# Edge rows of P by V stacked into shared groups, bounds moved between engines, first loads halved

## The chip, the cores and the metric

The kernel runs on one core of one Trainium2 chip. The time is that of one execution on the device, in microseconds (us), median of three runs. Engines are named as in the profile: PE (TensorE, matrix products, with PEld for its weight loads), DVE (VectorE), ACT (ScalarE), POOL (GpSimd) and SP (SyncE, which here only issues DMA transfers).

## The reference

Windowed attention with a few global tokens, then a two-layer network on its output. Batch 8, 8 heads, 512 local and 32 global tokens per batch, head width 64, model width 512, inner width 2048.

```
s_l = scale * concat(q_l k_g^T, where(|i-j| <= 32, q_l k_l^T, -1e9))
out_l = softmax(s_l) @ concat(v_g, v_l)
out_g = softmax(scale * q_g concat(k_g, k_l)^T) @ concat(v_g, v_l)
x = concat(out_g, out_l), heads side by side        # 8*544 tokens x 512
h = x @ w_in ;  g = h * tanh(softplus(h)) ;  out = g @ w_out
```

## The kernel before, in words

All large products are done in 16-bit pieces with float32 accumulation. An operand is scaled by a power of two, its high part is rounded to float16 and its low part (what is left) is a second float16; a product is then three 16-bit matmuls (high-high, high-low, low-high). The scale needs a bound on the operand, and each operand has its own way to get one: for W1 and W2 (`w_in`, `w_out`) PE sums squares by small products of a piece with itself into `w_s` (`w_stat`, L568); for V of batch 0, DVE takes the largest magnitude (`b_max`, L667 and L670); for V of later batches ACT sums magnitudes (L663). `w_bits` (L546 to L549) first rebuilds float32 words from the 64-bit words in which the weights come.

Attention goes by batch `b`, head pair `hp` and tile `t` of 128 query rows (four tiles for 512 rows). A tile needs keys of its own 128 rows, 32 rows on either side, and the 32 global rows. `scores` (L837) gives the products, `row_max` (L852, DVE) adds the mask and takes the row's largest, `expo` (ACT, L862 in batch 0, L865 with a row sum elsewhere) gives P. In batches from 1 on `p_hi` and `p_lo` split P into `ph`, a DMA transpose (`p_turn`, L637) writes `pt`, and `pv` (L954) multiplies `pt` by V: `vf` holds the tile's own V rows, `vb` the edge and global rows, which four small DMAs per head pair copy next to each other (`v_move`). Twelve matmuls serve a tile: two heads, two groups of rows, three products. In batch 0 PE itself transposes P (`p_pe`, L889, L897) and sums its rows by products with a column of ones (L960).

The network goes in 17 blocks of 256 tokens (two per batch, one for the global tokens) and 8 slices of the inner width: `h` (L1132 in block 0, L1142 after it), the function of h on ACT and DVE (`mish`, L1283 to L1293), its split into `GG` (L456, L1302), and the product with W2 into `o` (L1314, from block 4 on L1410). PSUM has two buffers for `h`: the third slice can start only when ACT has read the first. `w_split` (L456, L604) splits W1 and W2.

Nothing is scheduled on the chip: `Plan` lists all tasks, and a table `STEPS` gives the order in which they are written out, so each engine has one fixed order. `SECOND` lists the tasks that go to the second of two possible engines (mostly DVE in place of ACT). `FILL` says where unused products of a constant (`w_s<-consts`, L1721) are put ahead of a task; 73 stand in the program. All large DMAs, small moves and DMA transposes are issued by SP, in one order, from two helper lines (L445, L637). A tile is taken from a ring of buffers, in the order of the rings.

The lines that follow are those which the steps of the prediction touch.

Of the kernel before, what the change touches and what calls it, by code (L numbers as in the profile page):

```python
# [1800 lines left out]
```

## Time and profile before

| | us |
|---|---|
| median of three runs | 862.61 (862.17 to 863.95) |
| the profiled execution | 863.22 |
| its span in the trace | 861.4 |
| PE busy | 848.1 (98%) |
| DVE busy | 771.5 (90%) |
| ACT busy | 674.9 (78%) |
| POOL busy | 14.8 (2%) |

The span is what the trace covers; 1.8 us of the execution lie around it. A busy share is an average: an engine that is busy 78% of the span can be full in one stretch. The granted TensorE clock is 1.00 of full speed in all stretches read below. L numbers are lines of the kernel before.

### The profile page before, as it was taken

The numbers are of one execution on the slowest core, as the hardware profiler recorded it, in microseconds if no ns is written. First come the engines' busy times: TensorE is split into PE (matmuls) and PEld (weight loads), VectorE is DVE, ScalarE is ACT, GpSimd is POOL, SyncE is SP. The second block draws the span as 40 slices with busy tenths as digits, with TensorE's granted clock in tenths as the row PEclk, the third lists the DMA queues.
The fourth block names the chain that finished last, engine by engine and source line by source line (L and its number), as shares of the span: only waits on it lengthen the run. The fifth ranks groups of instructions, "written<-read, shape, count | busy, mean of one in ns | idle before, by whom it ended". The sixth has DMA issues, their size and how long they took to land.

```text
span 861.4 us, 23843 instructions
## 1 busy us (share of the span) xinstructions
PE 848.1 (98%) x9341; PEld 711.0 (83%) x9341; DVE 771.5 (90%) x2191; ACT 674.9 (78%) x1416; POOL 14.8 (2%) x29
## 2 busy tenths in 40 slices
PE   7999999999999999999999999999999999999998
PEld 5888866577777788888888888888888889888987
DVE  7999999998999999998999988899989998899771
ACT  5999998799998999987898888887687783444450
POOL 1010000000000000000000000000000000000000
PEclk9999999999999999999999999999999999999999
DMA  8889487878878586786766676677655454000001
GB/s 280 305 294 264 136 154 180 177 167 169 205 159 189 115 182 136 154 191 148 155 138 161 139 162 137 153 164 164 132 119 110 94 90 75 1 26 2 26 4 48
DMA packets 213841, 122.85 MB, mean 143 GB/s; under 512 B 172384, under 2 KB 181472, under 8 KB 213728
## 3 DMA queue, kind: packets, MB, share of 16 engines
q1 hardware_dynamic: 213728, 121.33, 60.6%
q8 instruction: 73, 1.20, 0.6%
q14 instruction: 40, 0.33, 0.1%
HBM read 65.84 MB, written 8.91 MB: 87 GB/s over the span
## 4 chain that ended last, share of the span: by engine, by line
PE 91%; DVE 4%; ACT 2%; DMA 2%; issue 1%; SPq 1%; DVEq 0%; ACTq 0%
PE h L1142 35%; PE o L1410 27%; PE o L1314 10%; PE U L954 5%; PE s L837 4%; PE h L1132 3%; PE h L1216 2%; PE g L1029 2%; PE gu L1090 1%; PE w_s L568 1%; DMA vl<-in_vm 1%; DMA wraw<-in_w 1%; DVE W L549 1%; DVE P L852 0%; SPq L445 0%
## 5 line engine op out<-in xcount | busy, mean ns | idle before, releaser
L1142 PE MATMUL h<-xx,W 128*128 128x256 f16 x2880 | 334.1, 273 | 0.8 <-ACT e L1283 0.8
L1142 PEld LDWEIGHTS <-W 128*128 128x128 f16 x2880 | 276.1, 98 | 37.6 <-issue 4.3
L1410 PEld LDWEIGHTS <-GG 128*128 128x128 f16 x2037 | 196.9, 98 | 23.1 <-issue 0.7
L1410 PE MATMUL o<-W,GG 128*128 128x256 f16 x1455 | 167.9, 273 | 0.0
L1302 DVE SCALAR_TENSOR_TENSOR GG<-e,c,GG 128x896 f16<-128x896 f32 (+1 forms) x129 | 134.5, 1047 | 6.3 <-ACT GG L456 5.0
L456 ACT ACTIVATE GG<-e,c 128x896 f16<-128x896 f32 (+1 forms) x103 | 98.9, 967 | 38.4 <-DVE e L1293 34.5
L1283 ACT ACTIVATE e<-h,c 128x512 f32<-128x512 f32 x128 | 85.8, 684 | 36.9 <-PE h L1142 23.7
L865 ACT ACTIVATE P<-P,nm 128x192 f32<-128x192 f32 (+1 forms) x224 | 102.4, 458 | 10.9 <-DVE nm L852 10.1
L852 DVE CUSTOM_DVE_ANT_0 P<-s,masks 128x192 f32<-128x192 f32 (+1 forms) x256 | 89.1, 366 | 6.9 <-PE s L837 6.3
L1314 PE MATMUL o<-W,GG 128*128 128x512 f16 x384 | 90.2, 379 | 0.0
L934 DVE SCALAR_TENSOR_TENSOR ph<-P,ph 128x384 f16<-128x384 f32 x168 | 69.2, 440 | 3.2 <-ACT ph L456 2.8
L954 PEld LDWEIGHTS <-pt 128*128 128x128 f16 (+1 forms) x1536 | 60.4, 98 | 10.0 <-issue 3.5
L1410 PE MATMUL o<-t,GG 128*128 128x256 f16 x582 | 67.8, 273 | 0.0
L1283 ACT ACT_TABLE_LOAD x49 | 62.9, 1283 | 5.6 <-DVE GG L1302 4.7
L1314 PEld LDWEIGHTS <-GG 128*128 128x128 f16 x384 | 35.3, 98 | 37.0 <-issue 1.6
L954 PE MATMUL U<-vf,pt 128*128 128x64 f16 x768 | 56.1, 193 | 0.0
L954 PE MATMUL U<-vb,pt 128*128 128x64 f16 (+1 forms) x768 | 55.9, 192 | 0.0
L1291 DVE TENSOR_TENSOR e<-e 128x256 f32<-128x256 f32 x104 | 43.5, 421 | 1.6
L865 ACT ACT_TABLE_LOAD x33 | 42.3, 1283 | 0.5
L865 ACT ACTIVATION_READ_ACCUMULATOR P<-P,nm 128x1 f32 x224 | 42.1, 188 | 0.0
L456 ACT ACTIVATE ph<-P 128x384 f16<-128x384 f32 (+1 forms) x101 | 38.9, 421 | 0.9 <-DMA pt<-ph 0.5
L696 ACT ACTIVATE mx<-mx 128x544 f32<-128x544 f32 x48 | 31.1, 648 | 9.3 <-DMA mx<-in_mxs 9.1
(231 smaller groups left out, 1242.3 us busy)
## 6 DMA issues: line engine op xcount, KB each, us to landing
mx<-in_mxs SPq DMA_DIRECT2D x48, 272.0 KB, 3.1
vl<-in_vm SPq DMA_DIRECT2D x32, 256.0 KB, 3.8
GG<-in_w SPq DMA_DIRECT2D x16, 512.0 KB, 6.8
out<-ob SPq DMA_DIRECT2D x32, 256.0 KB, 2.8
vm<-in_vm SPq DMA_DIRECT2D x28, 256.0 KB, 3.5
kr<-in_kt SPq DMA_DIRECT2D x24, 288.0 KB, 3.7
W<-in_w SPq DMA_DIRECT2D x12, 512.0 KB, 5.9
qr<-in_qt SPq DMA_DIRECT2D x24, 256.0 KB, 3.6
```

Of the source, the lines that this page charges most:

```text
L456: A.activation(out=dst, in_=src, func=AF.Copy, scale=c)
L837: T.matmul(X[s[h]][:, c], q[r, u * 128:(u + 1) * 128], k[r, c0:c0 + w], start=(i == 0), stop=(i == len(terms) - 1))
L852: pl.add(DVE, 76 + 1.04 * w, lambda: V.tensor_tensor_reduce(out=X[P][:, h, a:a + w], in0=X[s][:, c], in1=masks[:, m0:m0 + w], scale=-SCALE ...
L865: pl.add(ACT, 94 + 0.832 * w + 186, lambda: A.activation(out=X[P][:, h, a:a + w], in_=X[P][:, h, a:a + w], func=AF.Exp, bias=X[nm], scale= ...
L934: V.scalar_tensor_tensor(y, x, PSC, hi, ALU.mult, ALU.subtract)
L954: T.matmul(X[u][:, t, h, :], X[pt][:k, p * 4 + h * 2 + c, :], vx[:k, t, vl, h * 64:(h + 1) * 64], start=(n == 0), stop=(n == 5))
L1142: T.matmul(X[h][:, f * TB:(f + 1) * TB], wh(i, wl)[:, off:off + 128], x_[:, d, x, o:o + TB] if b else x_[:, d, 1, x * TB:x * TB + TB], sta ...
L1283: pl.add(ACT, 587, lambda: A.activation(out=X[e][:, 0:4].rearrange("p a n -> p (a n)"), in_=X[h], func=AF.Mish, bias=0.0, scale=X[c][:, 0: ...
L1291: pl.add(DVE, dve(256), lambda: V.tensor_tensor(x(5, 7), x(0, 5, 4), x(2, 3).broadcast_to([128, 2, 128]), ALU.add), r=[[e, 0], [e, 2], [e, ...
L1302: pl.add(DVE, dve(n, 1), lambda: V.scalar_tensor_tensor(gdst(blk, i, 1), gsrc(blk, i), X[c][:, 2:3], gdst(blk, i, 0), ALU.mult, ALU.subtra ...
L1314: T.matmul(X[o], GG[:, r, c + f * 2 + t, g, :], wh(8 + i, wl)[:, f * 512:(f + 1) * 512], start=(i == 0 and n == 0), stop=(i == NF - 1 and ...
L1410: T.matmul(X[o][:, :256], gx(i)[:, g, pos] if apart(blk, i) else GG[:, r, col, g, :], factor(kind, i, wl), start=(fresh_ and n == 0), stop ...
```

## The change

The tables `STEPS`, `SECOND` and `FILL` are new, so the whole order changes; 118 filler products in 24 places replace 73 in 15. Rings may hand out buffers in any order (`flex`). The parts:

1. In batches from 1 on, the first and the last tile (t = 0 and 3) have an edge on one side only. Their `ph` is laid out in 6 blocks of 128 columns in place of 8, the high and the low edge part share one block, and `pv` takes 10 matmuls in place of 12 (`stacked`). For that `vb` has ten slots, and `v_move` issues six more small DMAs per head pair of those batches.
2. The row sums of batch 0 come from ACT's exponentials (`accum_out`), not from PE.
3. W2's bound comes from ACT (`w_abs`, eight sums of magnitudes over 1024 columns), not from 64 PE products.
4. The bound of V of batch 0 comes from 17 PE products (`gram`), not from DVE.
5. The first loads of q, of k and of the masks are cut in two, and the first pieces go first.

```diff
+    CUT, MCUT = {"kn": 384, "qn": 256}, 224
...
+        cols = {None: slice(0, n), 0: slice(0, c), 1: slice(c, n)}[half]
+        pl.add(DMA, dma((cols.stop - cols.start) / 2), lambda: load(X[name][:, part, cols], src[b * HP + hp][:, cols]),
...
+    def w_abs(j):
+        x = ("wa", j)
+        pl.add(ACT, act(1024) + 93, lambda: A.activation(out=X[x].bitcast(F16), in_=wf2(j).bitcast(F32).rearrange("p r f -> p (r f)"), func=AF.Abs,
+                                                         bias=0.0, scale=1.0 / 1024, accum_out=X["wa8"][:, j - 8:j - 7]),
...
+    def w_stat(k):
+        if k >= 16:
+            if k % 2 == 0:
+                w_abs(k // 2)
+        else:
+            gram(lambda: wf(k), 4, 0, k == 15, [wkey(*HV[k])])
...
+        if not b:
+            x = ("vl", b, hp) if hp < HP else ("vgraw", b)
+            gram(lambda: X[x][:, :512] if hp < HP else X[x], 4 if hp < HP else 1, 1, hp == HP, [x])
...
+        ends = lambda r: X[vf][r, 0:4:3, 0]
+        mv(32, lambda: X[vb][64:128, 1:10:8], lambda: ends(LO), vf, [vb, 4])
+        mv(32, lambda: X[vb][0:64, 0:8:7], lambda: ends(HI), vf, [vb, 5])
+        mv(8, lambda: X[vb][64:96, 0], lambda: X[g][hp * 32:(hp + 1) * 32, 0], g, [vb, 6])
+        mv(8, lambda: X[vb][32:64, 9], lambda: X[g][hp * 32:(hp + 1) * 32, 0], g, [vb, 7])
+        mv(8, lambda: X[vb][96:128, 0], lambda: X[vf][0:32, 1, 0], vf, [vb, 8])
+        mv(8, lambda: X[vb][0:32, 9], lambda: X[vf][96:128, 2, 0], vf, [vb, 9])
...
     def expo(b, hp, t, h):
-        if not b:
+        if sums_by_pe(b, hp):
...
     def pieces(t, P, ph, part):
+        if t in (0, 3):
+            x = X[ph].rearrange("p a h k -> p (a h k)")[:, :768].rearrange("p (h k) -> p h k", h=2)
+            at = lambda lo: x[:, :, 0:192] if lo == (t == 3) else x[:, :, 192:384]
+            return [(X[P][:, :, 0:192], at(part), at(0))]
...
+    PE_SUMS = ()
...
     def p_turn(b, hp, t):
-        turn(256, lambda: X[pt], lambda: X[ph].rearrange("p a h k -> p (a h k)"), r=[ph], new=[("pt", pt)])
+        n = 6 if stacked(b, t) else 8
+        turn(32 * n, lambda: X[pt][:, :n], lambda: X[ph].rearrange("p a h k -> p (a h k)")[:, :n * 128], r=[ph], new=[("pt", pt)])
...
     def pv(b, hp, t):
+            if stacked(b, t):
+                v = lambda l: X[vf][:, t, l]
+                own, n = (0, 0) if t == 0 else (2, 9)
+                work = [(own, v(0)), (own, v(1)), (1, X[vb][:, 1 + 2 * t]), (1, X[vb][:, 2 + 2 * t]), (2 - own, X[vb][:, n])]
+                for h in range(2):
+                    for n, (c, vx) in enumerate(work):
+                        T.matmul(X[u][:, t, h, :], X[pt][:, h * 3 + c, :], vx[:, h * 64:(h + 1) * 64], start=(n == 0), stop=(n == 4))
+                return
...
-        (26,14), (41,9), (66,9), (80,5), (90,3), (97,8), (101,1), (145,1), (204,2), (216,2), (221,7), (235,6), (266,3), (299,2), (359,1)
+        (33,4), (54,2), (67,10), (84,3), (109,7), (120,1), (132,2), (136,1), (147,2), (166,9), (183,6), (200,4), (212,11), (224,1), (275,5), (288,8), (290,3),
```

The first place is the start of SP's queue, with the loads ahead of PE's first product. Before:

```order
1 L445 DMA consts<-in_consts 128x128
2 L445 DMA qn_0_108<-in_qt 128x512
3 L445 DMA kn_0_110<-in_kt 128x736
4 L445 DMA vl_0_112<-in_vm 128x512
5 L445 DMA vgraw_114<-in_vg 128x128
6 L445 DMA masks<-in_masks 128x672
7 L445 DMA vl_1_117<-in_vm 128x512
```

After, in the same place:

```order
1 L462 DMA qn_0_104<-in_qt 128x256
2 L462 DMA kn_0_106<-in_kt 128x384
3 L462 DMA masks<-in_masks 128x224
4 L462 DMA vl_0_109<-in_vm 128x512
5 L462 DMA consts<-in_consts 128x128
6 L462 DMA vl_1_113<-in_vm 128x512
```

The product of q and k now needs 128 and 192 KB in place of 256 and 368 KB, and the constants and the rest of the masks come later.

The second place is ACT at the end of block 0 of the network; `e_7` is the last slice of block 0, `wa` is the new sum of magnitudes of W2. Before:

```order
134 L1283 ACT_TABLE_LOAD
135 L1283 ACTIVATE e_5_1462<-h_5_1409,c_1237 128x512
136 L456 ACTIVATE GG<-e_5_1462,c_1237 128x4x128
137 L546 ACTIVATE W<-GG,two 128x1024
138 L456 ACTIVATE W<-W,sw 128x1024
139 L1283 ACTIVATE e_6_1482<-h_6_1443,c_1237 128x512
140 L546 ACTIVATE W<-GG,two 128x1024
141 L456 ACTIVATE GG<-e_6_1482,c_1237 128x4x128
142 L1283 ACTIVATE e_7_1509<-h_7_1474,c_1237 128x512
```

After:

```order
132 L563 ACTIVATE W<-GG,two 128x1024
133 L601 ACTIVATE wa_1390,w_a_1169<-W 128x1024
134 L1357 ACT_TABLE_LOAD
135 L1357 ACTIVATE e_5_1408<-h_5_1352,c_259 128x512
136 L563 ACTIVATE W<-GG,two 128x1024
137 L1357 ACTIVATE e_6_1424<-h_6_1384,c_259 128x512
138 L601 ACT_TABLE_LOAD
139 L601 ACTIVATE wa_1434,w_a_1169<-W 128x1024
140 L730 ACTIVATE mx_1_1350,mx_2_1331<-mx_1_1350 128x544
141 L601 ACTIVATE wa_1452,w_a_1169<-W 128x1024
142 L1357 ACT_TABLE_LOAD
143 L1357 ACTIVATE e_7_1511<-h_7_1414,c_259 128x512
```

The sums of W2's magnitudes and their table loads stand between the last slices, and the split of W and of GG moved to DVE or behind.

The third place is SP in the last batch, where `vb` is filled for one head pair (`vf`: its own V, `vgf`: the global rows) between the transposes. Before:

```order
476 L445 DMA vb_94<-vf_1_11174 32x768
477 L637 DMA_TRANSPOSE pt_0_3_11280<-ph_87 128x8x128
478 L445 DMA vb_94<-vgf_10978 32x2x256
479 L445 DMA vl_2_11299<-in_vm 128x512
480 L445 DMA vb_94<-vgf_10978 32x2x256
481 L445 DMA kr_3_11327<-in_kt 128x576
482 L445 DMA qr_3_11332<-in_qt 128x512
483 L445 DMA vb_94<-vf_1_11174 32x768
484 L637 DMA_TRANSPOSE pt_1_0_11430<-ph_88 128x8x128
```

After:

```order
639 L671 DMA_TRANSPOSE pt_1_3_11515<-ph_87 128x6x128
640 L462 DMA vb_91<-vgf_10802 32x128
641 L462 DMA vl_3_11537<-in_vm 128x512
642 L462 DMA vb_91<-vf_2_11401 32x128
...
645 L462 DMA vb_91<-vf_2_11401 64x2x128 x2
646 L671 DMA_TRANSPOSE pt_1_2_11575<-ph_86 128x8x128
647 L462 DMA vb_91<-vf_2_11401 32x768
648 L671 DMA_TRANSPOSE pt_2_0_11626<-ph_85 128x6x128
```

Two rows that read like 640 and 642 are left out here. Ten moves per head pair stand in the queue in place of four, and half of the transposes carry 6 blocks in place of 8.

## Rows read from the trace of the kernel before

**Rows 1.** The page: busy time, share of the span, instructions of each engine.

```profile
PE 848.1 (98%) x9341; PEld 711.0 (83%) x9341; DVE 771.5 (90%) x2191; ACT 674.9 (78%) x1416; POOL 14.8 (2%) x29
```

**Rows 2.** Windows: stretch, length, busy of each engine (instructions), clock, DMA share, GB/s.

```profile
20.00:60.00 40.00, 38.15 (x633) 32.37 (x632) 39.31 (x106) 38.02 (x87) 1.90 (x2) 1.00 0.92 314
60.00:800.00 740.00, 738.75 (x7938) 615.37 (x7933) 685.99 (x1957) 604.48 (x1265) 8.93 (x15) 1.00 0.64 139
...
80.00:100.00 20.00, 20.00 (x149) 17.32 (x148) 19.90 (x36) 19.53 (x29) 1.00 (x2) 1.00 0.63 182
```

**Rows 3.** Timeline of the start: start, us, engine, line, op, out<-in, count [idle before].

```profile
1.66 0.43 SPq L445 DMA_DIRECT2D kn<-in_kt  x1
...
5.40 1.76 PE L837 MATMUL s<-kn,qn 64*128 64x192 f32 x8 [5.40 <-DMA kn<-in_kt]
...
7.32 0.69 DVE L667 TENSOR_REDUCE vmx<-vl 128x1 f32<-128x512 f32 x1 [4.14 <-DMA vl<-in_vm]
...
8.64 0.80 ACT L862 ACTIVATE P<-P,nm 128x192 f32<-128x192 f32 x2 [6.63 <-DVE nm L852]
```

**Rows 4.** Timeline of PE, 18 to 30 us.

```profile
19.56 0.93 PE L1721 MATMUL w_s<-consts 128*128 128x224 bf16 x8
20.32 0.62 PE L889 MATMUL T<-consts,P 128*128 128x128 f32 x4
...
23.07 0.25 PE L954 MATMUL U<-vb,pt 128*128 128x64 f16 x3
23.16 0.24 PE L960 MATMUL w_s<-ones,pt 128*128 128x1 f16 x4
23.27 0.25 PE L954 MATMUL U<-vf,pt 128*128 128x64 f16 x3
...
26.82 0.39 PE L568 MATMUL w_s<-W 128*128 128x128 bf16 x4
27.05 0.60 PE L907 MATMUL Tx<-consts,x 128*128 128x128 f32 x4
```

**Rows 5.** ACT: exponentials without and with sums, a W split, table loads grouped.

```profile
12.52 1.22 ACT L862 ACTIVATE P<-P,nm 128x224 f32<-128x224 f32 x3
13.64 0.58 ACT L456 ACTIVATE pt<-T 128x512 f16<-128x512 f32 x1
...
101.30 2.17 ACT L456 ACTIVATE W<-W,sw 128x1024 f16<-128x1024 f32 x2
...
115.68 0.47 ACT L865 ACTIVATE P<-P,nm 128x224 f32<-128x224 f32 x1
...
116.14 1.13 ACT L456 ACTIVATE W<-W,sw 128x1024 f16<-128x1024 f32 x1
...
L1283 ACT ACT_TABLE_LOAD x49 | 62.9, 1283 | 5.6 <-DVE GG L1302 4.7 <-PE h L1142 0.2
```

**Rows 6.** Timeline where block 0 of the network ends: ACT, then PE.

```profile
93.26 0.70 ACT L1283 ACTIVATE e<-h,c 128x512 f32<-128x512 f32 x1
...
96.56 8.02 PE L1142 MATMUL h<-xx,W 128*128 128x256 f16 x72
104.41 1.89 PE L1314 MATMUL o<-W,GG 128*128 128x512 f16 x8
```

**Rows 7.** SP's queue, 120 to 160 us: first and last issue, a transpose, a move.

```profile
120.62 1.23 SPq L637 DMA_TRANSPOSE xx<-ph  x1
...
127.55 1.23 SPq L637 DMA_TRANSPOSE pt<-ph  x1
128.87 0.57 SPq L445 DMA_DIRECT2D vb<-vf  x1
...
158.18 2.79 SPq L637 DMA_TRANSPOSE pt<-ph  x2
```

**Rows 8.** PE's product of that transpose's output; DMA view: count, median us to landing.

```profile
132.79 0.26 PE L954 MATMUL U<-vf,pt 128*128 128x64 f16 x3
...
pt<-ph SPq DMA_TRANSPOSE x112, 3.6
```

More of the change, by code (lines that the diff above doesn't have):

```diff
@@ L274, in add @@
             k, sub = self._key(x)
+            self.users.setdefault(k, set()).add(n)
             st = self.state.setdefault(k, {})
@@ L297, in add @@
             self.base[k], self.alloc[k] = (old, {n}) if part else (set(), set())
-            if tag in self.last:
+            self.users.setdefault(k, set()).add(n)
+            if tag in self.flex:
+                self.born.setdefault(n, []).append(k)
+            elif tag in self.last:
                 after.add(self.last[tag])
@@ L305, in add @@
             k, sub = self._key(x)
+            self.users.setdefault(k, set()).add(n)
             st = self.state.setdefault(k, {})
@@ L326, in order @@
         self.fill = {steps[p]: k for p, k in self.FILL} if len(self.STEPS) == N else {}
-        seen = set()
+        seen, held = set(), {tag: [] for tag in self.flex}
         for n in steps:
             assert self.tasks[n][2] <= seen and self.tasks[n][3] <= seen
+            for k in self.born.get(n, ()):
+                before = held[k[0]]
+                assert len(before) < self.flex[k[0]] or self.users[before[-self.flex[k[0]]]] <= seen
+                before.append(k)
             seen.add(n)
@@ L558, in fresh, with norm_of @@
         return len(seen) == 1
-    def w_stat(k):
-        w = k // 16
-        def go():
-            u = wf(k).bitcast(BF16).rearrange("p (c two) -> p c two", two=2)
-            for c in range(4):
-                a = u[:, c * 128:(c + 1) * 128, 1]
-                T.matmul(X["ws"][:, w * 128:w * 128 + 128], a, a, start=fresh(), stop=(k % 16 == 15 and c == 3),
-                         skip_group_check=True)
-        pl.add(PE, mm(4, 131) + 12, go, r=[wkey(*HV[k])], w=[["ws", w]])
-    def w_norm(w):
-        m, p = ("wm", w), ("wp", w)
-        pl.add(DVE, 210, lambda: V.tensor_tensor_reduce(out=X["wd", w][:, 0, :128],
-                                                        in0=X["ws"][:, w * 128:w * 128 + 128], in1=ident, scale=1.0,
+    def norm_of(m, p, at):
+        pl.add(DVE, 210, lambda: V.tensor_tensor_reduce(out=X["wd", at][:, 0, :128],
+                                                        in0=X["ws"][:, at * 128:at * 128 + 128], in1=ident, scale=1.0,
@@ L583, in w_norm, with gram, go @@
         pl.add(DVE, 64, lambda: V.tensor_scalar(e(), e(), 1, None, ALU.logical_shift_right), w=[p])
         pl.add(DVE, 64, lambda: V.tensor_scalar(e(), e(), 0x1FC00000, None, ALU.add), w=[p])
+    def gram(x, n, at, last, r):
+        def go():
+            u = x().bitcast(BF16).rearrange("p (c two) -> p c two", two=2)
+            for c in range(n):
+                a = u[:, c * 128:(c + 1) * 128, 1]
+                T.matmul(X["ws"][:, at * 128:at * 128 + 128], a, a, start=fresh(), stop=last and c == n - 1, skip_group_check=True)
+        pl.add(PE, mm(n, 131) + 12, go, r=r, w=[["ws", at]])
@@ new lines, in w_norm @@
+    def w_norm(w):
+        p = ("wp", w)
+        if w:
+            m, unit = ("wm", w), 2048.0
+            pl.add(DVE, 66, lambda: V.tensor_reduce(out=X[m], in_=X["wa8"], axis=AX.X, op=ALU.max), r=["wa8"], new=[("wm", m)])
+            pl.add(POOL, 600, lambda: G.partition_all_reduce(X[p], X[m], 128, RED.max), r=[m], new=[("p2", p)])
+            pl.add(DVE, 64, lambda: V.tensor_scalar(X[p], X[p], TINY / unit, None, ALU.max), w=[p])
+        else:
+            unit = 1.0
+            norm_of(("wm", w), p, 0)
+        iv, sc = iw[:, w:w + 1], sw[:, w:w + 1]
@@ L589, in w_norm @@
             pl.add(DVE, 64, lambda: V.tensor_scalar(iww, iw[:, 0:1], iw[:, 1:2], 1.0 / GSC, ALU.mult, ALU.mult), r=[["iw", 0], ["iw", 1]], w=["iww"])
-        else:
-            pl.add(DVE, dve2(128, 1), lambda: V.tensor_scalar(isw, ident, sc, None, ALU.mult), r=["consts", ["sw", 0]], w=["isw"])
     parted = set()
-    PELO = ()
     def w_split(j):
@@ L602, in w_split @@
         pl.add([(ACT, act(1024, 1)), (DVE, dve2(1024, 1))], 0, lambda e: scaled(e, wh(j, 0), f, c), r=[k, ["sw", w]], w=[wslot(j)])
-        if j not in PELO:
-            pl.add(DVE, dve(1024, 1), lambda: V.scalar_tensor_tensor(wh(j, 1), f, c, wh(j, 0), ALU.mult, ALU.subtract),
-                   r=[k, ["sw", w], hi], w=[lo])
-            return
-        for n in range(2):
-            T_, q = ("wl", j, n), slice(n * 512, n * 512 + 512)
-            def go(T_=T_, q=q):
-                T.matmul(X[T_], isw, f[:, q], start=True, stop=False)
-                T.matmul(X[T_], nid, wh(j, 0)[:, q], start=False, stop=True)
-            pl.add(PE, mm(1, 2048) + mm(1, 512) + 100, go, r=[k, "isw", "ids", hi],
-                   new=[("h", T_)], rows=0.64)
-            pl.add(from_ps(512), 0, lambda e, T_=T_, q=q: copy(e, wh(j, 1)[:, q], X[T_]), r=[T_], w=[lo])
+        pl.add(DVE, dve(1024, 1), lambda: V.scalar_tensor_tensor(wh(j, 1), f, c, wh(j, 0), ALU.mult, ALU.subtract),
+               r=[k, ["sw", w], hi], w=[lo])
     LO, HI = slice(0, 64), slice(64, 128)
@@ L627, in pair, with plain_load, plain_keys @@
         return (kind, b, hp // 2), hp % 2
-    def plain_load(b, hp, kind, src, n):
+    CUT, MCUT = {"kn": 384, "qn": 256}, 224
+    def plain_load(b, hp, kind, src, n, half=None):
         name, part = pair(b, hp, kind)
-        pl.add(DMA, dma(n / 2), lambda: load(X[name][:, part, :n], src[b * HP + hp]), w=[[name, part]],
-               new=() if name in pl.place else [(kind, name)])
+        c = CUT[kind]
+        cols = {None: slice(0, n), 0: slice(0, c), 1: slice(c, n)}[half]
+        pl.add(DMA, dma((cols.stop - cols.start) / 2), lambda: load(X[name][:, part, cols], src[b * HP + hp][:, cols]),
+               w=[[name, (part, z)] for z in ((0, 1) if half is None else (half,))], new=() if name in pl.place else [(kind, name)])
+    def plain_keys(b, hp, kind, halves=(0, 1)):
+        name, part = pair(b, hp, kind)
+        return [[name, (part, z)] for z in halves]
     def turn(kib, dst, src, r, w=(), new=()):
@@ L840, in scores @@
             (q, part), (k, _) = pair(b, hp, "qn"), pair(b, hp, "kn")
-            pl.add(PE, sum(151 + 1.4375 * WIN[u][1] for u in ts) + 15, lambda: products([(X[q][:, part], X[k][:, part])]),
-                   r=[[q, part], [k, part]], new=new, rows=0.25)
+            pl.add(PE, sum(WIN[u][1] / 0.6 for u in ts) + 14, lambda: products([(X[q][:, part], X[k][:, part])]),
+                   r=plain_keys(b, hp, "qn", (t // 2,)) + plain_keys(b, hp, "kn", (0,) if t == 0 and not b else (0, 1)), new=new, rows=0.25, table="tile4")
             return
         qs, ks, kl = ("qs", b, hp), ("ks", b, hp), ("kl", b, hp)
-        pl.add(PE, sum(3 * (WIN[u][1] / 2.4 + 7) for u in ts) + 80, lambda: products(
-            [(X[qs][:, 0], X[ks]), (X[qs][:, 0], X[kl]), (X[qs][:, 1], X[ks])]), r=[qs, ks, kl], new=new, rows=0.6)
+        pl.add(PE, sum(3 * (WIN[u][1] / 2.4 + 2.6) for u in ts) + 10, lambda: products(
+            [(X[qs][:, 0], X[ks]), (X[qs][:, 0], X[kl]), (X[qs][:, 1], X[ks])]), r=[qs, ks, kl], new=new, rows=0.6, table="tile")
     def row_max(b, hp, t, h):
@@ L896, in p_pe @@
             return
-        pl.add(PE, mm(1, 517), lambda: T.matmul(X[T_], pid, flat(0), start=False, stop=True, skip_group_check=True), r=[pt, "ids"], w=[T_])
+        pl.add(PE, mm(1, 517), lambda: T.matmul(X[T_], pid(), flat(0), start=False, stop=True, skip_group_check=True), r=[pt, ("pid",)], w=[T_])
         cast(1)
@@ L956, in go @@
                         n += 1
-                if not b:
+                if sums_by_pe(b, hp):
                     for c in range(2):
@@ L961, in go @@
                                      skip_group_check=True)
-        pl.add(PE, mm(12, 69) + 14 if b else mm(20, 69), go, r=[pt, vb, vf] + ([] if b else ["ones"]), w=([] if head else [u]) + ([] if b else [["ws", ("sums", hp)]]),
-               new=[("u", u)] if head else ())
+        sums = sums_by_pe(b, hp)
+        pl.add(PE, mm(20 if sums else 10 if stacked(b, t) else 12, 69) + 14, go, r=[pt, vb, vf] + (["ones"] if sums else []),
+               w=([] if head else [u]) + ([["ws", ("sums", hp)]] if sums else []), new=[("u", u)] if head else ())
     def by_pe_sums(hp):
@@ L971, in x_norm @@
         if b:
+            pl.add(DVE, 73, lambda: V.tensor_scalar(X[rs][:, q], X[sums][:, q], EPS, PSC, ALU.add, ALU.mult), r=[sums], new=[("rs", rs)])
+        elif not sums_by_pe(b, hp):
             pl.add(DVE, 73, lambda: V.tensor_scalar(X[rs][:, q], X[sums][:, q], EPS, PSC, ALU.add, ALU.mult), r=[sums], new=[("rs", rs)])
@@ L1029, in go @@
                         T.matmul(X[g][64 * n:64 * n + 64, c0:c0 + w], x, rhs(k), start=(i == 0), stop=(i == last))
-        r = [[kn, kp] for kn, kp in plain] + [("qgraw", b)] if plain else [(x, b, hp + n) for n in range(2) for x in ("ks", "kl")] + [("qgh", b)]
-        ns = 2 * mm(1, 1050) + 230 if plain else mm(6, 262) + 3 * mm(1, 60) + 120
-        pl.add(PE, ns, go, r=r, rows=0.6 if plain else 1.0, new=bank(("g", b, hp, 0)) + bank(("g", b, hp, 1)))
+        r = [k for n in range(2) for k in plain_keys(b, hp + n, "kn")] + [("qgraw", b)] if plain else [(x, b, hp + n) for n in range(2) for x in ("ks", "kl")] + [("qgh", b)]
+        ns = 2 * mm(1, 1050) + 130 if plain else mm(6, 262) + 3 * mm(1, 60) + 34
+        pl.add(PE, ns, go, r=r, rows=0.6 if plain else 1.0, table="cols4" if plain else "cols", new=bank(("g", b, hp, 0)) + bank(("g", b, hp, 1)))
     def g_max(b, hp):
@@ L1723, in attn_mish_kernel @@
             pl.add(DMA, dma(64), lambda: load(ident, consts_in), w=["consts"], new=[("o", "ws")])
-            pl.add(DMA, dma(168), lambda: load(masks, masks_in), w=["masks"])
+            pl.add(DMA, dma(56), lambda: load(masks[:, :MCUT], masks_in[:, :MCUT]), w=["masks"])
+            pl.add(DMA, dma(112), lambda: load(masks[:, MCUT:], masks_in[:, MCUT:]), w=["masks1"])
         elif a == "g":
@@ L1728, in attn_mish_kernel @@
             b_load(0)
-    pl.add(DVE, dve2(128), lambda: V.tensor_scalar(pid, ident, -1.0 / PSC, None, ALU.mult), r=["consts"], w=["ids"])
+    pl.add(DVE, dve2(128), lambda: V.tensor_scalar(pid(), ident, -1.0 / PSC, None, ALU.mult), r=["consts"], new=[("qgh", ("pid",))])
     pl.add(DVE, dve2(128), lambda: V.tensor_scalar(nid, ident, -1.0, None, ALU.mult), r=["consts"], w=["ids"])
```

89 lines of the change are left out of this document (50 added, 39 removed), and 342 rows, old and new, of tables (SECOND, STEPS).

## The prediction

> **What bounds the kernel now.** I read the busy line first: PE is at work 98% of the span, DVE 90%, ACT 78% [rows 1]. The windows say where that average hides something. From 60 to 800 us PE is busy 738.75 of 740 us, so each matmul taken away there is worth its full length, as long as what PE waits for keeps up; DVE is busy 686 of these 740 us. From 20 to 60 us it is otherwise: PE 38.15 of 40, DVE 39.31, ACT 38.02; and from 80 to 100 us ACT has 19.53 of 20 us and DVE 19.90 while PE, too, is full [rows 2]. So the reader is to see two kernels: a first 100 us in which three engines are full at once, and a rest that PE alone bounds. At the very start PE waits until 5.40 us for k, DVE until 7.32 us for V, and ACT has nothing until 8.64 us, when DVE, which took V's maximum first, has the first row maxima [rows 3].
>
> **PE's work.** PE's matmuls overlap, so one costs the distance to the next start, not its shown duration. P by V: 3 in 0.09 us (23.07 to 23.16), 30 ns each; a product with ones: 4 in 0.11 us (23.16 to 23.27), 27.5 ns; a product for W's bound: 4 in 0.23 us, 57.5 ns; an unused filler: 8 in 0.76 us, 95 ns [rows 4].
> Removed: 7 batches x 4 head pairs x 2 tiles = 56 stacked tiles with two matmuls fewer, 112 x 30 ns = 3.4 us; 128 products with ones, 3.5 us; 64 products for W2's bound, 3.7 us. Added: 17 products for V's bound, 1.0 us; 45 fillers (118 less 73), 4.3 us. Net: -10.6 + 1.0 + 4.3 = -5.3 us. The fillers may fall into PE's idle time, of which 20 to 60 us has 1.85 us, so their cost lies between 2.4 and 4.3 us. I take 4.3, since the new order puts them among work.
>
> **The start.** PE's first product now waits for 128 + 192 = 320 KB instead of consts, q and k (64 + 256 + 368 = 688 KB). Before, k was issued at 1.66 us, third in the queue, and PE began 3.74 us later; now k is second, one issue of 0.43 us earlier. If the 3.74 us shrink with the bytes, PE begins at 1.23 + 3.74 x 320/688 = 3.0 us; if nothing is gained, at 5.4. I take 4.1, near the middle: 1.3 us earlier (0 to 2.4) [rows 3]. For DVE and ACT more goes: V's maxima no longer stand ahead of the row maxima. The first group of 8 matmuls takes 1.76 us, its first quarter 0.4, and a row maximum some 0.4 (an estimate from the exponentials of the same tile, below), so ACT begins at 4.9 to 6.3 in place of 8.64. I take a head start of 3.0 us for ACT (0, if it then waits for the halves that come later, to 3.7).
>
> **ACT until block 0 of the network is done.** That is where the removed work went. From the order, counted up to the last slice's function `e_7`: 8 sums over 1024 columns of W2 at 1.09 us (a W split of that size, 2.17 for two) = 8.7 us; 32 exponentials now with a sum, 0.46 us apart against 1.12/3 = 0.37, 0.09 each = 2.8 us; two table loads more, 1.28 each = 2.6 us; five splits of V of 512 columns at half a W split, 2.7 us. Gone to DVE or behind: three W splits 3.3 us, four GG casts 2.2 us, and eleven small instructions, while two come, nine at some 0.37 us = 3.3 us (an estimate, the exponential's length). Sum: 16.8 - 8.8 = +8.0 us [rows 5].
> Before, `e_7` ended at 93.96 us (93.26 + 0.70) and PE began the second slice of block 1 at 96.56; only two PSUM buffers hold h, so that slice needs the buffer that `e_7` read [rows 6]. This is a cover of 2.6 us. Now `e_7` ends at 93.96 + 8.0 - 3.0 = 99.0. PE comes there at 96.56 - 1.3 (start) + 0.5 = 95.8; the 0.5 is what its order has ahead of that place: -3.5 - 3.7 + 1.0 + 4.3 = -1.9, and 34 P-by-V and 15 global products of the same kind (1.5) and 4 score instructions (0.9, at two matmuls of h, 109 ns, each) that come earlier than before, +2.4. So PE stands 3.2 us, in one or two pieces.
>
> The Trainium skill ("ScalarE: Activation LUTs", section "What ACT_TABLE_LOAD costs") says that every switch pays a drain of about 1380 ns beside the 1283 ns of the load. The rows of 49 such loads show 1283 ns, and 5.6 us of idle time ahead of all of them together, 0.11 each, so a drain does not show as idle time here [rows 5]. By that rule the two added switches would cost 2.8 us more, and PE would stand 6.0 us in place of 3.2.
>
> **Until the product with W2, and after it.** This product began at 104.41 us [rows 6]. In the new order three slices of block 1 stand ahead of it, not four: 24 matmuls at 7.85/72 = 109 ns = 2.6 us go behind. PE's work up to it: +0.5 - 2.6 = -2.1 us. So it begins at 104.41 - 1.3 - 2.1 + 3.2 = 104.2, 0.2 earlier. From there PE has -5.3 + 2.1 = -3.2 us of work, in a stretch that PE fills [rows 2]. DVE takes over about 20 copies from ACT there, and keeps pace, having had 54 us to spare over these 740; I cost them at nothing. If that cover fails in some blocks, part of twenty copies of some 0.4 us, 8 us on DVE, comes through to PE; I allow 2 us for it.
> Span: 861.4 - 0.2 - 3.2 = 858.0. The profiled execution took 863.22, 1.8 more than its span, so 859.8; it was 0.6 above the median of 862.61, so **859.2 us**.
>
> **SP's queue.** Six moves more per head pair are 28 x 6 = 168 issues. One holds SP 0.57 us, so 96 us over some 620. From 120 to 160 us SP's 34 rows (37 issues) add up to 34.3 us of 40 [rows 7]. Smaller transposes give some back: two of four per pair carry three quarters, at most 0.3 us each. I cost this at nothing, by the time between a transpose's output and its use: issued at 127.55, landed after 3.6 us at 131.15, used at 132.79, 1.6 us later [rows 8]. The cover is gone when more than two or three moves stand ahead of a due transpose. Their sizes, 8 and 32 KB, take DMA time that no row shows: as bytes nothing (112 KB per pair, against 256 KB of one load), as packets up to the 48 KB move's full 2.9 us, which hides behind the same cover.
>
> The Trainium skill ("DMA: Bandwidth & Descriptors", section "Bandwidth") has it that transfers under 64 KB are dominated by their descriptors, which speaks against cutting rows out into moves of 8 KB. The row shows that a 48 KB move holds SP 0.57 us [rows 7]; what its descriptors cost the DMA engines no row shows.
>
> **Rivals.**
> - *A, the forecast*: ACT takes back part at the end of block 0. Own range 858 to 862: the head start 0 gives 862.2, 3.7 gives 858.5.
> - *B, the whole sum arrives.* If PE does not stand (the splits moved away let `e_7` come earlier, or the slices overlap otherwise), 859.2 - 3.2 = 856.0; with the idle 1.85 us of 20 to 60 gone too, 854.2. I set 855.5. For it: all three engines get work off where they are full. Against it: ACT's +8.0 stands in a stretch where it had 0.5 of 20 us free [rows 2].
> - *C, ACT's lag takes all.* The head start does not come: 859.2 + 3.0 = 862.2; and if each of the two added switches cost twice the 1.28 us of its load, 2.6 more, 864.8. I set 862.5. For it: DVE, too, has the row maxima, the row sums and moved copies there, and 39.31 of 40 us busy. Against: the first loads do get smaller.
> - *D, slower: SP's queue fills.* 34.3 us of 40, and 1.8 head pairs fall in 40 us, 11 moves x 0.57 = 6.2 less 1.0: 39.5. It decides from the point where SP has no free time: then each transpose waits behind moves of the next pair, past its 1.6 us. If the 12 pairs of batches 1 to 3 each lose one issue, 0.57 us, that is 7 us: 866. Against it: rows of two issues hold waits (two transposes in 2.79 us, 1.40 each against 1.23), so the queue has some slack inside its 34.3 us [rows 7].
>
> **Chances.** A 0.42, B 0.25, C 0.17, D 0.16. A difference under 0.2% (1.7 us) cannot be told from none here: faster is below 860.9, slower above 864.3. Of A 0.34 lies below 860.9, and all of B: faster 0.59. Same: 0.08 of A, 0.13 of C, 0.21. Slower: D and 0.04 of C, 0.20. The range must reach into B and D: 854 to 866.
>
> **What would show it.** Right: PE's first matmul near 4.1 us, ACT's first exponential at 5 to 6; a wait of PE for ACT's `e` between 92 and 100 us of some 3 us in all; the first product with W2 near 104; PE busy about 843 us; from 110 us on PE without gaps of more than before. B: no such wait, and that product near 101. C: the wait is 6 us or more. D: PE waits for `pt`, between 120 and 330 us, time after time, and SP without gaps. Wrong altogether: a stretch after 110 us in which PE waits for DVE, whose extra copies I cost at nothing.

## The result and the profile after

The changed kernel takes 873.39 us (872.67 to 874.9, four runs) against 863.28 for the one before: a ratio of 1.0119 (95% interval 1.0099 to 1.014), 10.1 us slower. The forecast was 859.2, range 854 to 866.

The page of the kernel after, busy time and the chain that ended last:

```profile
PE 849.2 (98%) x9099; PEld 705.9 (81%) x9099; DVE 777.7 (89%) x2214; ACT 679.5 (78%) x1443; POOL 18.6 (2%) x29
...
PE 57%; DVE 17%; ACT 10%; DMA 9%; issue 3%; SPq 3%; POOL 0%; ACTq 0%; DVEq 0%
```

PE was busy 848.1 us before [rows 1], and the forecast's sum had 843. The span grew by 9.5 us, more than PE's busy time, so PE also stands more: 21.7 us instead of 13.3. The chain, which before was 91% PE, now runs through DVE, ACT and DMA for 36% of the span: a step of PE often waits for something that itself came late.

The windows after (stretch, length, busy of PE, PEld, DVE, ACT, POOL, clock, DMA share, GB/s):

```profile
20.00:60.00 40.00, 37.69 (x511) 31.39 (x513) 37.77 (x108) 38.03 (x106) 0.00 (x0) 1.00 0.87 292
60.00:800.00 740.00, 731.43 (x7744) 604.30 (x7741) 687.86 (x1959) 604.51 (x1262) 14.39 (x17) 1.00 0.63 140
```

Against [rows 2], PE lost 7.3 us of its 740 in the long stretch (731.43 against 738.75), the stretch that had no gap to speak of. DVE, which has 23 instructions more, is busy 2 us more there, ACT the same: they are not fuller, they are late. What PE waited for in the whole span (us in total, times, longest):

```profile
PE s L878 <- DMA kn<-in_kt: 4.2, 2, 3.8
PE h L1216 <- ACT e L1357: 2.5, 5, 1.1
PE s L878 <- DVE nm L893: 2.2, 2, 1.1
PE U L1015 <- DMA pt<-ph: 1.6, 3, 1.2
PE w_s L595 <- DMA vl<-in_vm: 1.5, 3, 0.6
PE T L951 <- ACT pt L473: 1.1, 1, 1.1
```

There are many small waits for different things: `nm` (the row maxima) from DVE, `e` from ACT, `pt` from DMA. The timeline of SP suggests what they have in common, and the first experiment tests it. Around the longest wait for `pt` (start, us, issue):

```profile
222.94 0.56 SPq L462 DMA_DIRECT2D vb<-vf  x1
223.55 1.27 SPq L462 DMA_DIRECT2D vb<-vgf  x2
224.92 0.54 SPq L462 DMA_DIRECT2D vb<-vf  x1
...
227.60 1.25 SPq L671 DMA_TRANSPOSE pt<-ph  x1
228.91 1.35 SPq L462 DMA_DIRECT2D vb<-vgf  x2
230.37 1.28 SPq L671 DMA_TRANSPOSE pt<-ph  x1
231.69 1.55 SPq L462 DMA_DIRECT2D vb<-vf  x2
233.36 0.51 SPq L462 DMA_DIRECT2D vm<-in_vm  x1
233.98 1.24 SPq L671 DMA_TRANSPOSE pt<-ph  x1
```

And PE at the end of that wait:

```profile
239.04 0.23 PE L1015 MATMUL U<-vf,pt 128*128 128x64 f16 x2 [1.17 <-DMA pt<-ph]
```

In this stretch the queue has next to no free time: moves of `vb` stand between the transposes and the loads, each for some 0.6 us. The last transpose, with a 256 KB load just ahead of it, landed after 5.0 us, where the median is 3.4. Over longer times the queue is not full: in no stretch of 40 us between 80 and 720 us do SP's issues add up to more than 36.8. Half of the 112 transposes of `pt` now carry 6 blocks, and they hold SP 152.8 us in all, 153.0 before, so nothing is given back there. From 80 to 720 us the issues of SP add up to 479 us of 640, before to 372. Loads come late by the same queue: ACT's idle time ahead of the bounds of q and k (`mx`, L730) is 15.9 us, before (L696) 9.3.

The start after, at the places of [rows 3] and [rows 6] and between them (first PE, then DVE, then ACT):

```profile
3.76 1.75 PE L878 MATMUL s<-kn,qn 64*128 64x192 f32 x8 [3.76 <-DMA kn<-in_kt]
6.15 0.61 PE L595 MATMUL w_s<-vl 128*128 128x128 bf16 x4 [0.64 <-DMA vl<-in_vm]
...
8.24 1.30 PE L595 MATMUL w_s<-vl 128*128 128x128 bf16 x8 [0.62 <-DMA vl<-in_vm]
...
11.72 1.76 PE L878 MATMUL s<-kn,qn 64*128 64x224 f32 x8
...
62.88 1.91 PE L1206 MATMUL h<-xx,W 128*128 128x256 f32 x8
...
84.92 1.41 PE L1797 MATMUL w_s<-consts 128*128 128x224 bf16 x13
86.62 7.17 PE L1206 MATMUL h<-xx,W 128*128 128x256 f32 x32 [0.30 <-ACT e L1357]
...
97.40 2.78 PE L1216 MATMUL h<-xx,W 128*128 128x256 f16 x24
...
101.11 0.51 PE L1164 MATMUL gu<-gpt,vf 128*128 128x64 f16 x12
101.71 5.53 PE L1216 MATMUL h<-xx,W 128*128 128x256 f16 x48
107.08 5.34 PE L1388 MATMUL o<-W,GG 128*128 128x512 f16 x24
...
9.69 0.29 DVE L579 CUSTOM_DVE_ANT_0 wd<-w_s,consts 128x128 f32<-128x128 f32 x1 [2.16 <-PE w_s L595]
...
6.03 0.46 ACT L906 ACTIVATE P<-P,nm 128x192 f32<-128x192 f32 x1 [4.02 <-DVE nm L893]
...
11.83 0.60 ACT L473 ACTIVATE pt<-T 128x512 f16<-128x512 f32 x1 [3.01 <-PE T L943]
...
100.98 0.69 ACT L1357 ACTIVATE e<-h,c 128x512 f32<-128x512 f32 x1
```

The reader is to see that the first steps came as forecast, PE at 3.76 us and ACT at 6.03, and that nothing of it is left at 100 us: `e_7` ends at 101.67, the second slice of block 1 begins at 101.71 and the product with W2 at 107.08, where the forecast had 99.0, 99.0 and 104.2, and the kernel before 93.96, 96.56 and 104.41 [rows 6]. PE hardly waits for `e_7`: its work ahead of the second slice ends at 101.62 (101.11 + 0.51), 0.1 us before. The wait of some 3 us between 92 and 100 us that the forecast named as its sign is not there; PE is busy 8.00 of the 8 us from 92 to 100.

### The profile page after: what moved, and what is told of

It is laid out like the page before. It is cut to its first block, busy times and chain, and to the rows that moved or that the text cites. A ratio compares the mean times of both kernels' runs of the same rounds, so it can differ in the third digit from the quotient of the medians.

```text
span 870.9 us, 23633 instructions
## 1 busy us (share of the span) xinstructions
PE 849.2 (98%) x9099; PEld 705.9 (81%) x9099; DVE 777.7 (89%) x2214; ACT 679.5 (78%) x1443; POOL 18.6 (2%) x29
## 4 chain that ended last, share of the span: by engine, by line
PE 57%; DVE 17%; ACT 10%; DMA 9%; issue 3%; SPq 3%; POOL 0%; ACTq 0%; DVEq 0%
PE h L1216 22%; PE o L1484 20%; PE o L1388 5%; PE s L878 3%; DVE GG L1376 2%; SPq L462 2%; DVE P L893 2%; DMA mx<-in_mxs 2%; DMA pt<-ph 2%; DVE ph L988 2%; DMA vm<-in_vm 2%; PE h L1290 2%; PE U L1025 1%; ACT L1357 1%; ACT e L1357 1%
## 5 line engine op out<-in xcount | busy, mean ns | idle before, releaser
L906 ACT ACTIVATE P<-P,nm 128x192 f32<-128x192 f32 (+1 forms) x256 | 117.4, 460 | 9.6 <-DVE nm L893 8.5
L473 ACT ACTIVATE GG<-e,c 128x896 f16<-128x896 f32 (+1 forms) x94 | 90.6, 974 | 39.2 <-DVE e L1367 31.2
L906 ACT ACTIVATION_READ_ACCUMULATOR P<-P,nm 128x1 f32 x256 | 48.5, 190 | 0.0
L730 ACT ACTIVATE mx<-mx 128x544 f32<-128x544 f32 x48 | 31.2, 650 | 15.9 <-DMA mx<-in_mxs 15.8
L1364 DVE TENSOR_TENSOR e<-e 128x128 f32<-128x128 f32 x104 | 29.4, 286 | 15.2 <-ACT e L1357 12.5
L473 ACT ACTIVATE ob<-o,c 128x256 f32<-128x256 f32 (+1 forms) x42 | 21.0, 500 | 24.2 <-PE o L1484 23.6
L473 ACT ACTIVATE ph<-P 128x384 f16<-128x384 f32 (+1 forms) x95 | 36.8, 423 | 1.5 <-DMA pt<-ph 1.0
L878 PE MATMUL s<-ks,qs 64*128 64x192 f16 (+1 forms) x384 | 34.8, 252 | 2.3 <-DVE nm L893 2.2
```

The source lines that it names most:

```text
L473: A.activation(out=dst, in_=src, func=AF.Copy, scale=c)
L730: pl.add(ACT, act(544) + 93, lambda i=i, k=k: A.activation(out=X[k][:, :544], in_=X[k][:, :544], func=AF.Abs, accum_out=X[mx][:, i:i + 1]) ...
L878: T.matmul(X[s[h]][:, c], q[r, u * 128:(u + 1) * 128], k[r, c0:c0 + w], start=(i == 0), stop=(i == len(terms) - 1))
L906: pl.add(ACT, 94 + 0.832 * w + 186, lambda: A.activation(out=X[P][:, h, a:a + w], in_=X[P][:, h, a:a + w], func=AF.Exp, bias=X[nm], scale= ...
```

## The experiments

Two theories stood against each other. *Queue*: the 168 added issues fill SP's one in-order queue, and transposes and loads come late (the same queue as in the forecast's rival D). *Order*: the new order and the new split between DVE and ACT leave PE waiting. Times are medians; "before" ran beside each group on the same chip (863.1 to 863.7). The groups ran on different chips, so two runs of different groups are best compared by their ratios to "before"; a difference of two such ratios has an error of 1.3 to 1.6 us.

**1. The moves left out** (`e1_no_moves`).

```diff
-            pl.add(DMA, dma_on(kib), lambda: load(dst(), src()), ...)
+            pl.add(DMA, dma_on(kib), lambda: None if w[1] > 3 else load(dst(), src()), ...)
```

> The changed kernel (873.4) without the six added moves per head pair of batches 1 to 7; the slots they fill keep old or zero values, so the edge parts of tiles 0 and 3 are not computed fully. If SP's queue is the cause (168 issues of 0.57 us in one in-order queue make transposes and loads late), most of the 9.6 us of added PE stalls between 120 and 720 us goes: 863 to 866. If the new order and the new split of work between DVE and ACT are the cause, the stalls stay: 872 to 874.

864.44 us, ratio to before 1.0011 (1.0000 to 1.0022). 9 of the 10 us are gone, with the same order and the same work on PE, DVE and ACT. Order theory falls for these. From 110 us on only these waits of PE are left:

```profile
PE h L1290 <- ACT e L466: 1.0, 3, 0.5
PE h L1216 <- ACT e L1357: 0.6, 2, 0.4
```

The waits for `pt` and `nm` are gone, and ACT's idle time ahead of `mx` is 4.5 us, 15.9 with the moves: these did hang on the queue.

**2. Without stacking and moves** (`e2_unstacked`).

```diff
     def stacked(b, t):
-        return b > 0 and t in (0, 3)
+        return False
...
     def pieces(t, P, ph, part):
-        if t in (0, 3):
+        if False:
```

> The changed kernel with P by V of tiles 0 and 3 as before (12 matmuls, 8 blocks, no added moves), in the new order. By the PE sum it is 112 x 30 ns = 3.4 us longer than the kernel without the moves. Queue theory: 866 to 869, under the changed kernel. Order theory: 875 to 877, over it.

865.76 us, 1.0033 (1.0020 to 1.0046). So the 112 matmuls are worth 1.3 us by the medians, 1.9 by the ratios, where the sum had 3.4; with the error that is not clearly less. And whoever leaves out part 1 altogether is 7.6 us ahead of the change.

**3. The kernel before with the moves** (`e3_before_moves`, and a second version, `e3b_before_spare_moves`, whose edit is shown).

```diff
+            def go():
+                load(dst(), src())
+                n = w[1]
+                if b and n < 2:
+                    load(isw[n * 64:n * 64 + 64].bitcast(F16)..., X[vf][(1 - n) * 64:(1 - n) * 64 + 64, 0:4:3, 0])
+                if b:
+                    load(spare[n * 32:n * 32 + 32], src()[:, 0, 0])
```

> The kernel before (863.3) with six more small moves per head pair of batches 1 to 7, of 8 and 32 KB, issued by SP right behind the four it has; they write the same data again. Queue theory: the same damage as in the change, 868 to 874. Order theory: nothing, 863 to 865.

1067.07 us, 1.2362 (1.2319 to 1.2406), far beyond both theories. In this first version the added moves wrote to places that the move just ahead had written, and SP stood until that one had landed (205 us in 112 waits in the trace), so this run tells of such waits and not of the queue. The second version writes to spare places, as in the diff above.

> The kernel before (863.1) with six more small moves per head pair of batches 1 to 7, as in the change four of 8 KB and two of 32 KB, issued by SP right behind the four it has, now to spare memory, so that no move waits for another. Queue theory: 868 to 876. If the queue has room and only the place in the new order did the damage: 863 to 865.

907.48 us, 1.0506 (1.0466 to 1.0547): 44 us, in an order that was not made for them, and far more than the 868 to 876 expected. What PE waited for there:

```profile
PE U L962 <- DMA pt<-ph: 12.5, 6, 3.2
...
PE h L1150 <- ACT e L1291: 5.0, 8, 1.8
PE o L1418 <- ACT ob L457: 3.1, 1, 3.1
PE gu L1098 <- DMA gpt<-gph: 2.9, 4, 1.5
```

First `pt`, then `e` and others, as in the change. SP's issues from 80 to 720 us add up to 457 us here, less than in the change, and the loss is five times as large; so where the moves stand counts, and not only how many there are. That the new order kept the loss small by spreading them is likely, but no run shows it.

**4. The moves done elsewhere** (`e4_pool_moves`, `e8_moves_gpsimd_dma`).

```diff
-            ... lambda: load(dst(), src()), ...
+            ... lambda: G.tensor_copy(dst(), src()) if w[1] > 3 else load(dst(), src()), ...      # e4
+            ... lambda: (G if w[1] > 3 else nc.sync).dma_start(dst(), src()), ...                 # e8
```

> The changed kernel with the six added moves done by POOL as copies, which is busy 2% of the span, and not by SP. Queue theory: as without the moves, 863 to 866, as long as POOL's copies don't hold DVE. Order theory: 872 to 874.

866.95 us, 1.0044 (1.0028 to 1.0060). Better than the change, but 2.5 us over the run without moves. It goes with a slower DVE: POOL's copies (count, busy us, mean ns), then the page's busy line of this run:

```profile
L824 POOL COPY vb<-vf 64x256 f16<-64x256 f16 x56 | 33.5, 598 | 112.3 <-ACT vf L473 52.6 <-DVE vf L475 47.6 <-issue 9.5
...
PE 847.9 (98%) x9099; PEld 705.8 (82%) x9099; DVE 787.3 (91%) x2214; ACT 679.4 (78%) x1443; POOL 109.9 (13%) x197
```

DVE is busy 787.3 us with the same 2214 instructions that took 777.7 us in the change. That this is what costs the 2.5 us is argued, not shown.

> The changed kernel with the six added moves as the same DMAs, but issued by POOL and not by SP. If SP's issue time is what counts, 864 to 866, like without the moves (864.4). If the DMA engines' time for 168 small transfers counts, it stays at 871 to 874. A third way: POOL's issuing slows DVE as POOL's copies did (DVE 787 us busy there, 777 without): 866 to 868.

864.22 us, 1.0002 (0.9990 to 1.0015). The same 168 DMAs, the same bytes, only issued from POOL's queue:

```profile
vb<-vf POOLq DMA_DIRECT2D x56, 32.0 KB, 3.1
...
vb<-vgf POOLq DMA_DIRECT2D x56, 8.0 KB, 3.2
...
PE 847.3 (98%) x9099; PEld 706.0 (82%) x9099; DVE 777.8 (90%) x2214; ACT 678.6 (79%) x1443; POOL 108.7 (13%) x197
```

They land after 3.1 to 3.2 us, and DVE is not slowed (777.8 us). So it is SP's issuing and not the DMA engines' work. Nor do the moves hold SP by waiting for their own data: in the change's trace SP stood 6.9 us for that ahead of all its moves from 80 to 720 us, and 5.0 us in the run without the added ones.

**5. Two of the six moves** (`e10_two_of_six_moves`).

```diff
+            ... lambda: None if w[1] > 5 else load(dst(), src()), ...
```

> The changed kernel with the two added moves of 32 KB and without the four of 8 KB per head pair; 56 issues stay of 168, two thirds of the added bytes. By issues and a queue that is full at some points only, a third of the damage or less: 865 to 868. By bytes, two thirds: 870 to 871.

864.09 us, 1.0001 (0.9989 to 1.0013): no damage that can be told, with two thirds of the added bytes, and less than either expectation had. SP's issues from 80 to 720 us add up to 413 us of 640 here, 366 without the moves, 479 with all six. In this order the loss sets in between 65% and 75% of SP's time, long before the 100% on which rival D put its point. It is no fixed point: the second version of experiment 3 had 71% and lost 44 us.

**6. The start, one cost at a time** (all without the added moves, base 864.44).

```diff
+        self.fill = {}                                                       # e5
...
+            gram(lambda: X[pair(0, 0, "kn")[0]][:, 0, :384], ...)            # e6
...
+            out=X[x].bitcast(F16)[:, :64], in_=wf2(j)...[:, :64], func=AF.Abs   # e7
...
+        go = lambda: load(X[name][:, part, :n], ...) if half == 0 else None ...  # e9
```

> The changed kernel without the six added moves (864.4) and without any of the 118 fillers. If fillers cost PE what they take and stand among work in the start, the 15.4 us that they hold PE (before: 8.7 us for 73) come back in part: 857 to 861. If they stand where PE would wait for DVE and ACT, nothing changes: 863 to 866; and if PE works at the lower pace without them (its first matmuls after a rest took twice as long), slower.

864.46, no change. The page's busy line of this run:

```profile
PE 838.9 (97%) x8981; PEld 697.4 (81%) x8981; DVE 777.7 (90%) x2214; ACT 679.4 (79%) x1443; POOL 18.6 (2%) x29
```

Without 118 fillers PE is busy 7.1 us less than in the run without moves (846.0), and the time is the same: most fillers stand where PE would wait. But the run changes a second thing. Where 13 fillers stand in the change at 84.92 us, PE now rests, and is slower after it:

```profile
85.97 12.31 PE L1206 MATMUL h<-xx,W 128*128 128x256 f32 x48 [1.95 <-ACT e L1357]
```

In the run without moves, 48 such products in a row took 10.63 us. The granted clock, 1.00 there, is 0.96 from 20 to 60 us and 0.86 from 80 to 92 us here: around 54 us and around 89 us it is 0.50, 1.2 GHz in place of 2.4. So what the fillers cost and what they keep in clock may cancel in part; this run can't part the two.

> The changed kernel without the six added moves (864.4), with V's bound of batch 0 taken from the part of k that is there first, so PE's 17 products don't wait for V's loads (they held PE from 6 to 10 us with four waits). If that wait in PE's order costs the start, 861 to 863; if DVE and ACT bound the start, 864 to 865.

862.36, ratio 0.9986 (0.9976 to 0.9995): 2.1 us come back, more than the error.

> The changed kernel without the six added moves (864.4), ACT's eight sums for W2's bound over 64 columns and not 1024 (the bound is too small by chance, the order the same). It takes about 0.8 us from each, 6.4 us of ACT before and in block 0. ACT lag theory (the forecast's 3.2 us of waiting): 861 to 862. If PE's own list and DVE set the start: 864 to 865.

863.00, ratio 0.9998 (0.9988 to 1.0008): 1.4 us less, 1.1 by the ratios, which is within the error.

> The changed kernel without the six added moves (864.4), the first loads of q, k and the masks whole, at the place of their first pieces. The forecast gave the halves 1.3 us at PE and 3.0 us at ACT. If that head start reaches the end: 866 to 868; if it is lost again in the start, where V's loads come next: 864 to 865; below 864 if the later pieces were what came late.

864.39, ratio 1.0012 (0.9998 to 1.0026), no change: the halved loads bring nothing to the end.

**7. Two attempts on the start together** (on the kernel with POOL's issues, 864.22).

```diff
+        first = [5, 3, 1, 4, 6, 2, 0, 8, 9, ..., 175, 176, ..., 194, 195, 196, 209, 210, ..., 37, 38, 190, 39, 200, 40, 41]
+        steps = first + [n for n in steps if n not in set(first)]            # e11; e12 is e6 and e7 together
```

> The changed kernel with the six added moves issued by POOL (864.2), and the start reordered: the second pieces of k, q and the masks are loaded ahead of V, the scores and row maxima of tiles 2 and 3 and their exponentials stand ahead of V's bound on PE, DVE and ACT. If PE's wait for V's loads, with the second scores behind it, is what ate the head start (2.1 us came back when the bound didn't wait), 861 to 863. If V's bound, now some 1.4 us later, is itself what the start waits for, 864 to 866.

866.18, 1.0029 (1.0020 to 1.0039), 2 us slower: V's bound, put later, is itself waited for (DVE stands 4.6 us for PE's products of the bound, in the change 2.2).

> The changed kernel with the moves issued by POOL, V's bound taken from k, and W2's eight sums over 64 columns: both costs of the start taken away at once. If the two are separate parts of one chain through the start (2.1 and 1.4 us when taken alone), 860 to 861.5; if ACT's work only counts where PE waits for V, 862 to 863; if the forecast's whole sum for PE arrives once both are gone, 855 to 857.

863.27, 0.9994 (0.9983 to 1.0004): 1.0 us less than its base, not 3.5. As far as the error lets one tell, the two costs don't add up.

**8. DVE's load, and the weights' loads** (`e13`, `e14`, `e15`, `e16`, `e17`).

```diff
+               ... V.scalar_tensor_tensor(f()[:, :, :64], words(j)[:, :, :64, 1], 3, ...)    # e13, e14
...
+            ... (G if w[1] > 3 or not b else nc.sync).dma_start(dst(), src())               # e15
+            ... G.dma_start(dst(), src())                                                   # e16
+            ... (nc.sync if b else G).dma_start(dst(), src())                               # e17, in the kernel before
```

> The changed kernel with the moves issued by POOL (864.2), DVE's 32 instructions that rebuild the weights over 128 columns and not 1024 (1.22 us each; the weights are wrong). That takes some 32 us from DVE before 100 us and leaves PE's list as it is. If DVE (with ACT behind it) bounds the start, so that PE's removed work was worth nothing there, it falls far: 845 to 856. If PE's list or the loads bound the start: 862 to 864.

> The kernel before (863.3) with the same cut. By the same theory it falls, too, 848 to 858, and now PE's own list is nearer to the bound: the changed one, with 7.2 us less of needed work on PE in the start and 3.4 later, should then be ahead of it by 2 to 6 us, where with all of DVE's work it is 1 us behind. If the two fall alike and stay 1 us apart, PE's list is not what counts there even then.

In both, the rebuilding of the weights' words covers 128 columns of 1024. 863.59 and 862.82, both within the error of their bases. The page's busy line of the first:

```profile
PE 845.2 (98%) x9099; PEld 705.2 (82%) x9099; DVE 750.2 (87%) x2214; ACT 678.4 (79%) x1443; POOL 106.3 (12%) x197
```

DVE has 28 us less to do here (27 in the other), and the time doesn't move in either kernel: DVE alone does not bound the start.

> The changed kernel with the six added moves and also all moves of batch 0 issued by POOL. In SP's order W1's 16th load stands behind the last moves of batch 0, which wait 6.5 us for V's low part (48.81 us, against 46.06 before), with DMA at 251 to 299 GB/s in the stretches where it had 304 to 347. If that head-of-line wait for weights is what bounds the start, the first matmul with W1 comes 2 to 6 us earlier than 63.1 us, and the time is 858 to 862. If W1's loads are held by the buffers they go to, or the start by V's bound, 863 to 865.

> As the run with batch 0's moves issued by POOL, and the other four per head pair, too: 280 issues fewer for SP than the changed kernel has. Queue theory: the same as that run or up to 2 us less, 857 to 862; if POOL's own order of 280 moves makes V's edge rows late, more: 864 to 868.

> The kernel before with batch 0's moves issued by POOL. Its W1 loads stand behind the same moves (SP waits 4.2 us for V's low part there). If weights behind moves bound its start as well, 859 to 862; if only the new order suffers from it, 863 to 864.

863.54, 863.71 and 863.44, all the same as before within the error. In the first, the weights came earlier (DMA moved 397 GB/s from 10 to 20 us and 360 from 20 to 30, in its base 252 and 323) and the first matmul with W1 began at 61.5 us in place of 63.1; at most 0.7 us of that reached the end. The theory that the weights' waiting behind moves bounds the start falls as well.

No version that computes all its parts beats the kernel before.

## Why the prediction was wrong

**The queue** is the step that failed: "I cost this at nothing, by the time between a transpose's output and its use". It cost 9.0 us (873.4 to 864.4 without the moves, 864.2 with the moves issued by POOL). The rival was there, with 7 us and 0.16; I gave it little because 39.5 of 40 us still seemed to fit. The mistake is in the measure, for the queue did its damage well before it was full: at 413 us of 640 nothing was lost, at 479 some 9 us, and the fullest 40 us held 36.8. In the stretch that I had read, 120 to 160 us, SP's issues alone add up to 31.5 us before and 31.0 after; the added ones stand elsewhere. And I looked only at the transposes: I expected waits of PE for `pt` between 120 and 330 us, time after time, and found 2.0 us of these in the whole span, beside waits for `nm` that went with the moves, too, and late loads (`mx`) in the same queue. The sign that was to speak against DVE's extra copies, PE waiting for DVE after 110 us, came, too (2.2 us for `nm`), but it goes away with the moves, so costing these copies at nothing held. Rival D had the right cause, but neither its condition nor its sign came. (The six moves carry 96 KB per head pair, not the 112 that I wrote; nothing hangs on it.)

**The head start of 3.0 us** was the second: 0 at the end (the run with whole loads: no change). The first steps came as forecast, but PE's 17 products for V's bound, which I priced at 57.5 ns each and not as waits, stand ahead of the second scores, for loads that land one after the other. These began at 11.72 us; in the kernel before:

```profile
9.82 1.59 PE L837 MATMUL s<-kn,qn 64*128 64x224 f32 x8
```

ACT stands 3.01 us for PE until 11.83, and that is its head start gone.

**ACT's lag** was right as a sum of work and wrong as a wait. Up to the end of `e_7` ACT did 89.1 us of work, 81.2 before: 8.0 us more, as summed. It stood 12.5 us up to there, 12.8 before, so nothing of the head start is left, and `e_7` ends at 101.67, where the forecast's own working with a head start of 0 gives 102.0. But the forecast had PE ready for the second slice at 95.8, and PE came there at 101.6. That both are late by about as much is why the product with W2 still comes where this working puts it (107.2, measured 107.08); that is luck. PE's rows before, to compare:

```profile
60.24 1.99 PE L1132 MATMUL h<-xx,W 128*128 128x256 f32 x8
...
92.85 1.47 PE L1142 MATMUL h<-xx,W 128*128 128x256 f16 x12
```

PE is 2.6 us behind at its first product with W1 (62.88, before 60.24), 4.6 at the first slice of block 1 (97.40, 92.85), 5.2 at the second. Where ACT's `e` does hold PE is inside block 0: 13 fillers and 0.30 us of standing from 84.92 to 86.62 us, 1.95 us without the fillers. Its price in the time is not 3.2 us: six of the eight microseconds of ACT taken away brought 1.4 at most.

**PE's sum.** The removed W2 products and row sums (7.2 us) lie in the start, and no run shows them in the time. All 118 fillers can be taken out there without effect, so the 4.3 us for more of them can't be seen in it either, with the clock as a second cause in that run. Behind the start the sum holds, as the split below shows.

**Put together**, by the traces: the span is 870.9 us, and the forecast's was 858.0. Split at the first product with W2 (us from the start, and from there to the end):

| | to the product | from it on |
|---|---|---|
| forecast | 104.2 | 753.8 |
| before | 104.41 | 757.0 |
| the change | 107.08 | 763.8 |
| the change, moves issued by POOL | 107.70 | 754.8 |

Of the 12.9 us that the forecast missed, 10.0 lie behind that product, and 9.0 of these go with the moves' issues. The other runs bear this out. Eleven of the changed kernel's order have stacked tiles, at most two of the six added moves on SP, no copies by POOL and no reordered start: their second part takes 753.1 to 755.3 us. In the kernel before and its two versions without added moves it takes 757.0 to 757.6. So about the 3.2 us that the sum saves there do arrive. But the eleven reach the product only at 105.7 to 108.2 us, the three at 103.4 to 105.1. Without the queue's damage the start loses about what the rest gains, and so none of these versions beats the kernel before.

**What stays open**: what bounds the first 100 us. Fillers, DVE's work, V's wait, ACT's sums, the weights' waiting behind moves were each taken away; each gave 0 to 2.1 us. That PE, DVE, ACT and DMA are all near full there, so that each cut meets the next limit, fits all of these, but no run shows it.
